# Linear attention and a two-layer feed-forward kernel: weight loads in another order, the first quarter of w_in used earlier, stage two reordered, q of batch 3 loaded two units later

## The chip, the core and the metric

The kernel runs on one core of a Trainium2 chip. Times are device microseconds of one execution. Five engines work side by side: TensorE (PE, matmuls; its weight loads are the row PEld), VectorE (DVE), ScalarE (ACT), GpSimd (POOL) and SyncE (SP). Here POOL issues nearly all loads, SP issues the DMA transposes and some of the stores. The metric is the time of the whole kernel, the median of the runs shown.

## What is computed

```python
def _attn_ref(q, k, v, g_norm):                      # batch 8, heads 8, sequence 576, head_dim 64
    kv = np.einsum('bhsd,bhse->bhde', k, v)
    out = np.einsum('bhsd,bhde->bhse', q, kv)
    rms = np.sqrt(np.mean(out * out, axis=-1, keepdims=True) + 1e-06)
    return (out / rms * g_norm).astype(np.float32)

def _moe_ref(x, w_in, w_out, alpha):                 # 4608 tokens, d_model 512, d_ff 2048
    h = x @ w_in
    g = np.maximum(h, 0.0) + alpha * np.minimum(h, 0.0)
    return (g @ w_out).astype(np.float32)

x = attn_out.transpose(0, 2, 1, 3).reshape(4608, 512)  # the attention's output is the input of the second part
```

All inputs and the output are float32; the kernel computes with float16 operands.

## The kernel before

**Tiling.** The 4608 tokens are cut into nine windows of 512 tokens (`NW = 9`, `W = 512`). A batch has 576 tokens, so windows and batches do not coincide. In each window the first matrix product has 16 groups (128 columns of w_in each, four matmuls of 512 tokens, `m1_mm`, L600). A group's result h in PSUM goes through ACT (`m1_neg`, L609) and DVE (`m1_sum`, L615), which together make the activation and leave it in SBUF as `gt`. The loop over windows 1 to 8 runs 16 units, one per group; other work is hung on unit numbers by tables.

**The second matrix product.** In window 0 it is plain: `y_run(a, (g,))` adds group g to token tile a (one matmul of 512 columns, L643). From window 1 on, the product with w_out is done in seven products of half size (Strassen's scheme in the form of Winograd): `X_LIST` holds products 1 and 2, `YZ_LIST` 6, 7, 4, 5 and 3. They need sums of blocks of `gt` (`s_sum`, DVE, the tables `S_ONE`, `S_TWO`, `S_ALL`, `S_LST` say in which unit) and sums of blocks of w_out (`w_sum`, DVE, made once). `X_AT`, `X_1`, `X_LAST`, `YZ_AT`, `YZ_1` say how many of the product matmuls (L796) are issued in each unit.

**Start and stage two.** Until about 18 us the kernel makes the attention of batch 0 for window 0, one pair of heads after the other: transpose q (`step_t`), make kv (`step_kv`), multiply (`step_ot`), sum the squares by a matmul (`ssq_mm`), scale (`norm`). `keep_warm` issues matmuls whose result nobody reads. The first group's matmuls for the first chunk of x (`m1_parts`) are already issued in between. Then come the 16 groups of window 0, then stage two: the y matmuls of window 0 in an order written out by hand, mixed with the attention of batch 1 (for window 1), with the scaling of w_in by g_norm (`scale_w_in`, needed from window 1 on) and with `w_sum`. [...]

**Rows.** From window 2 on, the attention of the next window is made by rows while a window runs: `rows_mm` (L499) multiplies for a tile of 128 tokens, `rows_sq`, `rows_rs` (ACT) and `rows_norm` (DVE, L580) scale it, and SP transposes the tile into `xt` by a DMA (L585). For tile 2 of window 2 a version by columns is used (`cols_mm`, `cols_norm`, L541), which needs no transpose. `ROW_AT[w]` gives the units, while window w-1 runs: `kv`, `mm`, the eight `sq`, and per tile `rs` and `norm`. A window's unit 0 issues its four matmuls first for the tokens of tiles 0 to 2 (384 columns, `m1_cols`, L631), then the other four for tile 3.

**Loads.** POOL issues the loads of weights, k, v and q. The DMA semaphores of this queue are a ring of eight: an issue waits until the load eight places ahead of it has landed. At the start the order of loads is written out by hand (`load0`, `load_w_in`, `load_w_out`, `load_main`, `load_rem`). w_in comes in six pieces (`IN_CUTS`): pieces 0 to 3 have 256 columns (groups 0 and 1, 2 and 3, 4 and 5, 6 and 7), pieces 4 and 5 have 512 (groups 8 to 11, 12 to 15); w_out comes in eight pieces of two groups each. Later loads hang on units by `LOADS`: for window w the tuple `q, k, v` gives the unit in which batch w+2 is loaded, and a `gate` makes POOL wait for the activation of the group of the unit before. So `(11, 1, 1)` for w = 1 means: k and v of batch 3 in unit 1 of window 1, q of batch 3 in unit 11 behind a gate on group 10. Batch 3's q is loaded by four issues of 128 KB (`load_q`) and one for the remaining 64 rows; SP transposes it (`dma_t`, L380) in unit 0 of window 2.

Of the kernel before, what the change touches and what calls it, by code (L numbers as in the profile page):

```python
# [9 lines left out]
FP32 = mybir.dt.float32  # L10
FP16 = mybir.dt.float16
# [6 lines left out]
def kernel(  # L18
# [11 lines left out]
    nc = tc.nc  # L30
# [5 lines left out]
    P = 128  # L36
# [186 lines left out]
    def load_w_in(i):  # L223
        f0, f1 = IN_CUTS[i], IN_CUTS[i + 1]
        t = w_p.tile([P, NC, f1 - f0], FP16, name=f"w_in_sb{i}")
        src = moe_w_in[:, f0:f1].rearrange("(c p) f -> p c f", p=P)
        for c in range(0, NC, NC // 2 if i == 0 else NC):
            n = NC // 2 if i == 0 else NC
            nc.gpsimd.dma_start(out=t[:, c : c + n, :], in_=src[:, c : c + n, :])
        w_in_sb.append(t)  # L230
# [38 lines left out]
    load0("k", 3)  # L269
    load0("v", 3)  # L270
    load_w_in(0)
    load_w_in(1)
    load_w_in(2)
    load_w_in(3)
    load_w_in(4)
    load_w_in(5)
    load_w_out(0)
    load_main(1, "k")
    load_w_out(1)
    load_rem(1, "k")  # L280
# [8 lines left out]
    load_rem(1, "q")  # L289
    load_w_out(6)  # L290
    load_w_out(7)

# [563 lines left out]
    X_AT = [0, 0, 0, 4, 1, 1, 1, 3, 1, 3, 2, 0, 2, 2, 1, 7, 2, 2]  # L856
    X_1 = [0, 0, 0, 0, 0, 0, 1, 0, 4, 0, 0, 0, 7, 4, 6, 8, 0, 2]
    X_LAST = [0, 0, 0, 2, 1, 2, 0, 1, 1, 1, 1, 0, 3, 4, 0, 0, 0, 0]
    YZ_AT = [3, 7, 6, 5, 5, 6, 7, 4, 5, 7, 5, 4, 5, 6, 5, 0]
    YZ_1 = [0, 8, 8, 5, 7, 4, 7, 5, 4, 6, 4, 6, 6, 5, 5, 0]  # L860
# [77 lines left out]
    keep_warm(1)  # L938
    norm(0, 1)
    step_kv(0, 3)  # L940
# [9 lines left out]
    first = [ps_h.tile([P, W], FP32, name="h_ps", tag="h1")]  # L950
    first += [ps_o.tile([P, W], FP32, name="h_ps", tag="o") for g in range(2)]
    ssq_mm(0, 2, h_at(0))
    for g in range(2):
        m1_parts(g, 0)
# [62 lines left out]
    y_run(2, (4,))
    scale_w_in(4, 3, 4, nc.scalar)
    scale_w_in(4, 1, 4, nc.scalar)
    scale_w_in(1)  # L1020
    scale_w_in(3)
    y_run(3, (6,))
    scale_w_in(2)
    y_run(2, (5,))
    step_t(1, 2, S_POOL)
    y_run(1, (7,))
    y_run(2, (6,))
    y_run(1, (6,))
# [18 lines left out]
    ssq_mm(1, 1, Q_POOL)
    y_run(0, (6,))
    y_run(0, (9,))
    norm(1, 0)  # L1050
    y_run(3, (9,))
# [38 lines left out]
    y_out(ys[1], 0, 1)  # L1090
    step_t_rem(1, Q_POOL)
# [23 lines left out]
    def row_kv(bs):  # L1115
# [26 lines left out]
        2, 3, 4, 5, 6, 8, 9), 'rs': (5, 5, 9, 12), 'norm': (5, 6, 9, 12), 'red': (0, 0, 0, 1)}}  # L1142
# [166 lines left out]
```

## Time and profile before

| what | us |
|---|---|
| runs shown: median (lowest to highest of 3) | 274.43 (274.05 to 274.45) |
| the profiled execution | 274.92 |
| its span, first to last instruction | 273.1 |
| PE busy | 265.7 (97%) |
| DVE busy | 217.3 (80%) |
| ACT busy | 156.4 (57%) |
| POOL busy | 87.6 (32%) |

The mean granted TensorE clock is 0.999. All times inside the kernel are counted from the start of the span. In the views by stretches a line has the stretch, its length, the busy time and number of instructions of PE, PEld, DVE, ACT and POOL, then the granted clock, the DMA share and the GB/s. In the timeline a line has start, length, engine, line of the kernel, operation, output and inputs, shape and count, and in brackets the idle time ahead of it and what ended it. Matmuls are pipelined: a 512-column matmul is shown as 0.38 us long, while the next one starts 0.216 us after it. In the list of DMA issues a line has the queue, the kind, the number of issues, the KB of each and the time from the issue to the landing of its last part.

### The profile page before, as it was taken

Reading aid. Unit: us, or ns where it says so; the run is one execution under the profiler, and the core shown is the slowest. Engines: PE = TensorE matmul, PEld = TensorE weight load, DVE = VectorE, ACT = ScalarE, POOL = GpSimd, SP = SyncE. Lnnn points to the kernel's source line nnn. Section 1 sums busy time; section 2 is a strip of 40 time slices with the busy share of each in tenths; the row PEclk is TensorE's granted clock in tenths of the full one; section 3 lists DMA queues with packets and bytes.
Section 4 is the critical chain, followed back from the end, with each engine's and each line's share of the span. In section 5 each row is a group of like instructions: output and inputs, shape, how many; then the busy total and the mean of one; then the engine's idle time right before and its main releaser. Section 6 shows DMA issues by size and latency. Waiting matters only on the chain.

```text
span 273.1 us, 6175 instructions
## 1 busy us (share of the span) xinstructions
PE 265.7 (97%) x2286; PEld 168.5 (62%) x2286; DVE 217.3 (80%) x413; ACT 156.4 (57%) x532; POOL 87.6 (32%) x134
## 2 busy tenths in 40 slices
PE   7899999999799999999999999999999999999995
PEld 3354444456566676666666666676666666666684
DVE  6459658999768986998699869986998889778964
ACT  3467576785468546764675468546854864443410
POOL 8773461606251545154514341440110011101100
PEclk9999999999999999999999999999999999999999
DMA  8999999999989899959995999595051122211123
GB/s 160 197 202 202 195 199 193 178 182 108 161 159 204 132 166 148 153 113 172 135 144 130 151 135 158 137 143 111 19 134 43 41 44 90 61 40 40 40 77 119
DMA packets 91571, 35.59 MB, mean 130 GB/s; under 512 B 62980, under 2 KB 89748, under 8 KB 91540
## 3 DMA queue, kind: packets, MB, share of 16 engines
q0 software_dynamic: 57872, 23.83, 69.1%
q1 hardware_dynamic: 32628, 10.34, 22.4%
q10 hardware_dynamic: 1040, 1.02, 1.2%
q8 instruction: 18, 0.29, 0.4%
q14 instruction: 13, 0.11, 0.2%
HBM read 36.71 MB, written 9.44 MB: 169 GB/s over the span
## 4 chain that ended last, share of the span: by engine, by line
PE 79%; DMA 14%; DVE 2%; issue 1%; POOL 1%; ACT 1%; POOLq 0%
PE h_ps L600 35%; PE yY L796 15%; PE yZ L796 9%; PE yX L796 9%; DMA w_out_sb<-in_moe_w_out_dram 5%; PE y L643 4%; DMA xt<-x_rows 4%; DMA w_in_sb<-in_moe_w_in_dram 3%; DMA qst<-in_q_dram 2%; PE h_ps L631 2%; PE kv_ps L1122 2%; PE or_ps L499 2%; DVE gt L615 1%; DVE x_rows L580 1%; PE yZ L791 1%
## 5 line engine op out<-in xcount | busy, mean ns | idle before, releaser
L600 PE MATMUL h_ps<-xt,w_in_sb 128*128 128x512 f16 x540 | 136.2, 379 | 0.0
L609 ACT ACTIVATE m_sb<-h_ps 128x512 f32<-128x512 f32 x144 | 86.7, 603 | 81.9 <-PE h_ps L600 61.4
L615 DVE SCALAR_TENSOR_TENSOR gt<-m_sb,beta_sb,h_ps 128x512 f16<-128x512 f32 x144 | 106.2, 743 | 24.1 <-ACT m_sb L609 21.3
L600 PEld LDWEIGHTS <-w_in_sb 128*128 128x128 f16 x540 | 51.2, 98 | 39.4 <-issue 0.2
L655 POOL DMA_DIRECT2D out_dram<-y_sb x32 | 20.6, 646 | 123.3 <-DVE y_sb L838 57.1
L796 PEld LDWEIGHTS <-s 128*128 128x128 f16 x496 | 48.3, 98 | 11.3 <-DVE s L733 0.3
L796 PEld LDWEIGHTS <-gt 128*128 128x128 f16 x384 | 37.5, 98 | 23.2 <-issue 0.2
L796 PE MATMUL yX<-w_out_sb,gt 128*128 128x256 f16 x256 | 44.6, 273 | 0.0
L796 PE MATMUL yY<-wsum,s 128*128 128x256 f16 x256 | 35.2, 273 | 0.0
L562 ACT ACTIVATE sq_sb<-or_ps 128x64 f16<-128x64 f32 x144 | 30.9, 256 | 2.6 <-PE or_ps L499 2.6
L562 ACT ACTIVATION_READ_ACCUMULATOR sq_sb<-or_ps 128x1 f32 x144 | 30.3, 242 | 0.0
L580 DVE TENSOR_TENSOR x_rows<-or_ps,rstd_r 128x512 f16<-128x512 f32 x27 | 18.4, 684 | 1.0 <-ACT rstd_r L572 1.0
L828 DVE TENSOR_TENSOR u<-yY,p 128x512 f32<-128x512 f32 x16 | 11.0, 689 | 9.0 <-PE yY L796 9.0
L185 POOL DMA_DIRECT2D qst<-in_q_dram x20 | 17.7, 901 | 1.0 <-issue 1.0
L796 PE MATMUL yY<-wsum,gt 128*128 128x256 f16 x128 | 17.6, 272 | 0.0
L796 PE MATMUL yZ<-wsum,s 128*128 128x256 f16 x120 | 17.5, 272 | 0.0
L796 PE MATMUL yZ<-w_out_sb,s 128*128 128x256 f16 x120 | 16.7, 273 | 0.0
L643 PE MATMUL y<-w_out_sb,gt 128*128 128x512 f16 x64 | 16.3, 379 | 0.1
L731 DVE TENSOR_TENSOR s<-gt 128x512 f16<-128x512 f16 x32 | 13.3, 418 | 0.1
L733 DVE TENSOR_TENSOR s<-s,gt 128x512 f16<-128x512 f16 x32 | 12.8, 420 | 0.4
L737 DVE TENSOR_TENSOR s<-gt,s 128x512 f16<-128x512 f16 x32 | 12.7, 418 | 0.0
L735 DVE TENSOR_TENSOR s<-gt 128x512 f16<-128x512 f16 x32 | 12.4, 417 | 0.0
(107 smaller groups left out, 233.1 us busy)
## 6 DMA issues: line engine op xcount, KB each, us to landing
out_dram<-y_sb POOLq DMA_DIRECT2D x16, 256.0 KB, 2.7
kst<-in_k_dram POOLq DMA_DIRECT2D x7, 512.0 KB, 8.0
vst<-in_v_dram POOLq DMA_DIRECT2D x6, 512.0 KB, 7.9
qst<-in_q_dram POOLq DMA_DIRECT2D x20, 128.0 KB, 4.5
w_out_sb<-in_moe_w_out_dram POOLq DMA_DIRECT2D x8, 256.0 KB, 10.9
out_dram<-y_sb SPq DMA_DIRECT2D x5, 256.0 KB, 2.6
w_in_sb<-in_moe_w_in_dram POOLq DMA_DIRECT2D x2, 512.0 KB, 9.9
qst<-in_q_dram POOLq DMA_DIRECT2D x2, 512.0 KB, 11.9
```

Source lines behind the costliest of these rows:

```text
L185: nc.gpsimd.dma_start(out=st[:, t, :, :], in_=srcs["q"][b, :, t * P : (t + 1) * P, :].rearrange("h p d -> p h d"),)
L562: nc.scalar.activation(out=sq[:, half, j], in_=o_ps[:, half, j], func=AF.Square, accum_out=ssq[:, half, j : j + 1],)
L580: nc.vector.tensor_tensor(out=xr[:].rearrange("p j h d -> p h j d"), in0=o_ps, in1=rstd[:].unsqueeze(3).to_broadcast([P, 2, NPAIR, D]), op ...
L600: nc.tensor.matmul(out=h_ps[:], lhsT=w_in_blk(c, g), rhs=xts[w][:, c, :], start=(c == 0), stop=(c == NC - 1),)
L609: nc.scalar.activation(out=neg[w, g][:], in_=h_ps[:], func=AF.Relu, scale=-1.0)
L615: nc.vector.scalar_tensor_tensor(out=gts[w, i][:, r, :], in0=neg.pop((w, g))[:], scalar=beta_sb[:, g : g + 1], in1=h_ps[:], op0=ALU.mult, ...
L643: nc.tensor.matmul(out=y[:], lhsT=gt_cols(w, g, a * P, (a + 1) * P), rhs=w_out_blk(g), start=(n == 1), stop=(n == NF),)
L655: engs[store_turn[0] % len(engs)].dma_start(out=dst, in_=src)
L731: nc.vector.tensor_add(out=t[:], in0=a21, in1=a22)
L733: nc.vector.tensor_sub(out=t[:], in0=sums[w, 1, k][:], in1=a11)
L737: nc.vector.tensor_sub(out=t[:], in0=a12, in1=sums[w, 2, k][:])
L796: nc.tensor.matmul(out=bank, lhsT=lhs, rhs=rhs, start=fresh, stop=(c == NK - 1), skip_group_check=True,)
```

## The change

- `load_w_in` takes the range of w_in's four row chunks that it loads. Piece 0 is loaded in three parts instead of two halves: the first quarter (chunk 0) goes between k and v of the last pair of batch 0 (pair 3), then chunk 1, then chunks 2 and 3.
- In the list of loads w_out's piece 0 goes ahead of w_in's piece 3, the remainder of k of batch 1 ahead of w_in's piece 5, and the remainder of q of batch 1 behind the last pieces of w_out.
- One `keep_warm(1)` is taken out. The two matmuls `m1_parts(1, 0)` go ahead of `step_kv(0, 3)`, in its place; `m1_parts(0, 0)` stays behind `ssq_mm(0, 2)`.
- Stage two: the same y matmuls, attention steps, scalings and sums in another order. Two of the three transposes that stood together stay together, the third and the fourth stand alone.
- Other unit numbers in the tables of products (`X_AT`, `X_1`, `X_LAST`, `YZ_AT`, `YZ_1`), of sums (`S_ONE`, `S_TWO`, `S_ALL`, `S_LST`) and of rows: in window 2's rows `norm` of tile 0 goes from unit 4 to 5, tile 2's `rs` from 10 to 11 and its `norm` from 13 to 14; in window 8's rows both `mm` go from unit 1 to 0; for windows 4 to 7 `rs` of tile 1 goes from 8 to 7.
- `LOADS`: q of batch 3 in unit 13 of window 1 instead of 11, its gate on group 12 instead of 10.

```diff
--- before.py
+++ after.py
@@ -220,14 +220,12 @@
     GW = NF // WQ
     IN_CUTS = [i * FW // 2 for i in range(4)] + [i * FW for i in range(2, WQ + 1)]
 
-    def load_w_in(i):
+    def load_w_in(i, cs=(0, NC)):
         f0, f1 = IN_CUTS[i], IN_CUTS[i + 1]
-        t = w_p.tile([P, NC, f1 - f0], FP16, name=f"w_in_sb{i}")
+        if cs[0] == 0:
+            w_in_sb.append(w_p.tile([P, NC, f1 - f0], FP16, name=f"w_in_sb{i}"))
         src = moe_w_in[:, f0:f1].rearrange("(c p) f -> p c f", p=P)
-        for c in range(0, NC, NC // 2 if i == 0 else NC):
-            n = NC // 2 if i == 0 else NC
-            nc.gpsimd.dma_start(out=t[:, c : c + n, :], in_=src[:, c : c + n, :])
-        w_in_sb.append(t)
+        nc.gpsimd.dma_start(out=w_in_sb[i][:, slice(*cs), :], in_=src[:, slice(*cs), :])
 
     def scale_w_in(i, h=0, n=1, eng=None):
         f = (IN_CUTS[i + 1] - IN_CUTS[i]) // n
@@ -267,17 +265,19 @@
     load0("k", 2)
     load0("v", 2)
     load0("k", 3)
+    load_w_in(0, (0, 1))
     load0("v", 3)
-    load_w_in(0)
+    load_w_in(0, (1, 2))
+    load_w_in(0, (2, 4))
     load_w_in(1)
     load_w_in(2)
+    load_w_out(0)
     load_w_in(3)
     load_w_in(4)
+    load_rem(1, "k")
     load_w_in(5)
-    load_w_out(0)
     load_main(1, "k")
     load_w_out(1)
-    load_rem(1, "k")
     load_main(1, "q")
     load_w_out(2)
     load_w_out(3)
@@ -286,9 +286,9 @@
     load_main(1, "v", HH, H)
     load_w_out(4)
     load_w_out(5)
-    load_rem(1, "q")
     load_w_out(6)
     load_w_out(7)
+    load_rem(1, "q")
 
     warm_ps = ps_q.tile([P, W], FP32, name="warm_ps", tag="q")
 
@@ -853,11 +853,11 @@
         return [(n, a * NK + c) for n in ns for c in range(NK) for a in range(2)]
 
     X_LIST, YZ_LIST = products(1, 2), products(6, 7, 4, 5, 3)
-    X_AT = [0, 0, 0, 4, 1, 1, 1, 3, 1, 3, 2, 0, 2, 2, 1, 7, 2, 2]
-    X_1 = [0, 0, 0, 0, 0, 0, 1, 0, 4, 0, 0, 0, 7, 4, 6, 8, 0, 2]
-    X_LAST = [0, 0, 0, 2, 1, 2, 0, 1, 1, 1, 1, 0, 3, 4, 0, 0, 0, 0]
-    YZ_AT = [3, 7, 6, 5, 5, 6, 7, 4, 5, 7, 5, 4, 5, 6, 5, 0]
-    YZ_1 = [0, 8, 8, 5, 7, 4, 7, 5, 4, 6, 4, 6, 6, 5, 5, 0]
+    X_AT = [0, 0, 0, 4, 1, 2, 1, 2, 0, 4, 2, 0, 2, 2, 1, 7, 2, 2]
+    X_1 = [0, 0, 0, 0, 0, 0, 1, 0, 4, 0, 0, 0, 6, 5, 6, 8, 0, 2]
+    X_LAST = [0, 0, 0, 2, 1, 2, 0, 0, 1, 2, 1, 0, 3, 4, 0, 0, 0, 0]
+    YZ_AT = [3, 7, 6, 5, 5, 6, 7, 4, 5, 7, 5, 4, 5, 7, 4, 0]
+    YZ_1 = [0, 9, 7, 5, 7, 4, 7, 4, 5, 6, 4, 6, 7, 5, 4, 0]
     YZ_WHAT = ("u2", "u3", "c21", "c22", "c12")
 
     def x_prods(w, u):
@@ -935,9 +935,7 @@
     ssq_mm(0, 1, h_at(2))
     step_t(0, 3, h_at(1), nc.vector.tensor_copy)
     step_ot(0, 2, (ps_y, "y"))
-    keep_warm(1)
     norm(0, 1)
-    step_kv(0, 3)
 
     def m1_parts(g, c, parts=(0, 1)):
         for i in parts:
@@ -947,11 +945,15 @@
                 start=(c == i == 0), stop=(c == NC - 1), skip_group_check=True,
             )
 
-    first = [ps_h.tile([P, W], FP32, name="h_ps", tag="h1")]
-    first += [ps_o.tile([P, W], FP32, name="h_ps", tag="o") for g in range(2)]
+    first = [
+        ps_h.tile([P, W], FP32, name="h_ps", tag="h1"),
+        ps_o.tile([P, W], FP32, name="h_ps", tag="o"),
+        ps_o.tile([P, W], FP32, name="h_ps", tag="o"),
+    ]
+    m1_parts(1, 0)
+    step_kv(0, 3)
     ssq_mm(0, 2, h_at(0))
-    for g in range(2):
-        m1_parts(g, 0)
+    m1_parts(0, 0)
     step_ot(0, 3, Q_POOL, 2)
     first.append(ps_s.tile([P, W], FP32, name="h_ps", tag="s"))
     norm(0, 2)
@@ -987,124 +989,124 @@
         for g in gs:
             y_mm(ys[a], 0, a, g)
 
+    y_run(3, (1,))
     y_run(0, (0,))
-    y_run(2, (0,))
-    y_run(3, (1,))
     y_run(1, (1,))
-    y_run(3, (2,))
     y_run(3, (3,))
     y_run(1, (2,))
     y_run(3, (0,))
+    scale_w_in(0)
     y_run(0, (1,))
-    scale_w_in(0)
     y_run(2, (2,))
+    y_run(2, (0,))
     y_run(2, (1,))
     w_sum(1, 0)
     y_run(0, (2,))
+    w_sum(1, 1)
+    y_run(1, (3,))
+    y_run(3, (2,))
+    step_t(1, 0, O_POOL)
+    step_t(1, 1, Q_POOL)
     y_run(2, (3,))
+    y_run(0, (3,))
     scale_w_in(4, 0, 4, nc.scalar)
     y_run(1, (0,))
-    w_sum(1, 1)
-    y_run(1, (3,))
-    y_run(0, (3,))
-    step_t(1, 0, S_POOL)
-    step_t(1, 1, Q_POOL)
     step_t(1, 3, O_POOL)
     y_run(3, (4,))
+    step_t(1, 2, S_POOL)
     y_run(0, (5,))
+    y_run(2, (4,))
+    scale_w_in(4, 3, 4, nc.scalar)
+    scale_w_in(2)
+    scale_w_in(1)
+    y_run(3, (5,))
+    y_run(2, (5,))
...
-    S_ALL = [(2, -1, 3, 0), (2, -1, 3, 1), (3, -1, 3, 2), (8, -1, 4, 2), (9, -1, 4, 3), (4, -1, 4,
-        0), (14, 0, 2, 0), (12, 0, 1, 1), (13, 0, 2, 1), (11, 0, 1, 0), (4, -1, 4, 1), (3, -1, 3,
-        3), (16, -1, 1, 3), (0, -1, 2, 2), (16, -1, 2, 3), (14, 0, 1, 2)]
-    S_ONE = [(6, 0, 3, 0), (11, 0, 3, 3), (13, 0, 3, 2), (4, 0, 3, 1)]
+    S_ALL = [(2, -1, 3, 0), (2, -1, 3, 1), (3, -1, 3, 2), (11, -1, 4, 3), (4, -1, 4, 0), (14, 0, 2,
+        0), (4, -1, 4, 1), (13, 0, 2, 1), (11, 0, 1, 0), (3, -1, 3, 3), (8, -1, 4, 2), (16, -1, 1,
+        3), (0, -1, 2, 2), (12, 0, 1, 1), (16, -1, 2, 3), (14, 0, 1, 2)]
+    S_ONE = [(7, 0, 3, 0), (13, 0, 3, 2), (10, 0, 3, 3), (4, 0, 3, 1)]
     S_TWO = [(2, -1, 4, 2), (0, -1, 1, 1), (0, -1, 1, 0), (0, -1, 2, 1), (16, -1, 1, 2), (0, -1, 2,
-        0), (16, -1, 2, 2), (16, -1, 1, 3), (12, 0, 1, 0), (4, -1, 4, 0), (6, -1, 4, 1), (9, -1, 4,
+        0), (16, -1, 2, 2), (16, -1, 1, 3), (12, 0, 1, 0), (3, -1, 4, 0), (6, -1, 4, 1), (9, -1, 4,
         3), (12, 0, 2, 0), (15, 0, 2, 1), (14, 0, 1, 2), (16, -1, 2, 3), (12, 0, 1, 1)]
     S_LST = [(0, -1, 2, 2), (2, -1, 3, 0), (9, 0, 3, 2), (2, -1, 3, 1), (3, -1, 3, 2), (6, -1, 4,
         0), (5, -1, 3, 3), (6, 0, 3, 0), (12, 0, 1, 1), (9, 0, 3, 1), (12, -1, 4, 2), (12, -1, 4,
-        3), (13, 0, 2, 0), (6, -1, 4, 1), (13, 0, 2, 1), (10, 0, 1, 0), (14, 0, 1, 2), (14, 0, 2,
-        2), (11, 0, 3, 3), (16, -1, 1, 3), (16, -1, 2, 3)]
+        3), (13, 0, 2, 0), (6, -1, 4, 1), (10, 0, 1, 0), (14, 0, 1, 2), (14, 0, 2, 2), (11, 0, 3,
+        3), (16, -1, 1, 3), (13, 0, 2, 1), (16, -1, 2, 3)]
 
     def unit_sums(w, u):
         at = S_ONE if w == 1 else S_TWO if w == 2 else S_LST if w == NW - 1 else S_ALL
@@ -1136,13 +1138,13 @@
                 )
 
     ROW_AT = {2: {'kv': 5, 'mm': {0: ((0,),), 7: ((1, 3),), 8: ((2,),)}, 'sq': (1, 1, 7, 7, 8, 10,
-        7, 8), 'rs': (3, 9, 10, 9), 'norm': (4, 9, 13, 9), 'red': (1, 1, 0, 1)}, 3: {'kv': 0, 'mm':
+        7, 8), 'rs': (3, 9, 11, 9), 'norm': (5, 9, 14, 9), 'red': (1, 1, 0, 1)}, 3: {'kv': 0, 'mm':
         {4: ((1, 0),), 5: ((3, 2),)}, 'sq': (4, 4, 5, 6, 8, 8, 8, 9), 'rs': (6, 6, 10, 11), 'norm':
-        (6, 7, 10, 11), 'red': (0, 0, 1, 0)}, 8: {'kv': 99, 'mm': {1: ((1, 0), (3, 2))}, 'sq': (1,
+        (6, 7, 10, 11), 'red': (0, 0, 1, 0)}, 8: {'kv': 99, 'mm': {0: ((1, 0), (3, 2))}, 'sq': (1,
         2, 3, 4, 5, 6, 8, 9), 'rs': (5, 5, 9, 12), 'norm': (5, 6, 9, 12), 'red': (0, 0, 0, 1)}}
     for w in range(4, B):
         ROW_AT[w] = {'kv': 2, 'mm': {4: ((1, 0), (3, 2))}, 'sq': (4, 4, 5, 6, 7, 7, 8, 10), 'rs':
-            (6, 8, 9, 11), 'norm': (6, 8, 9, 11), 'red': (0, 0, 1, 0)}
+            (6, 7, 9, 11), 'norm': (6, 8, 9, 11), 'red': (0, 0, 1, 0)}
     COL_TILES = ((2, 2),)
     ROWS = {"sq": rows_sq, "rs": rows_rs, "norm": rows_norm}
     COLS = {"sq": cols_sq, "rs": cols_rs, "norm": cols_norm}
@@ -1187,7 +1189,7 @@
 
     LOADS = {}
     for w in range(1, B - 2):
-        q, k, v = (11, 1, 1) if w == 1 else (12, 3, 5)
+        q, k, v = (13, 1, 1) if w == 1 else (12, 3, 5)
         for nm, at in (("q", q), ("k", k), ("v", v)):
             when = LOADS.setdefault((w + at // NF, at % NF), [])
             if at > 1 or w == 1:
```

More of the change, by code (lines that the diff above doesn't have):

```diff
@@ L1003 @@
     y_run(0, (2,))
+    w_sum(1, 1)
[3 more added lines that the diff above has]
+    step_t(1, 1, Q_POOL)
     y_run(2, (3,))
+    y_run(0, (3,))
     scale_w_in(4, 0, 4, nc.scalar)
     y_run(1, (0,))
-    w_sum(1, 1)
-    y_run(1, (3,))
-    y_run(0, (3,))
-    step_t(1, 0, S_POOL)
-    step_t(1, 1, Q_POOL)
     step_t(1, 3, O_POOL)
     y_run(3, (4,))
+    step_t(1, 2, S_POOL)
     y_run(0, (5,))
+    y_run(2, (4,))
[4 more added lines that the diff above has]
+    y_run(2, (5,))
+    scale_w_in(3)
+    y_run(2, (7,))
+    y_run(3, (6,))
+    scale_w_in(4, 1, 4, nc.scalar)
+    y_run(1, (6,))
+    y_run(1, (7,))
+    y_run(2, (6,))
     y_run(0, (4,))
     y_run(1, (4,))
[L1017 to L1028, printed above, removed]
+    step_kv(1, 0, O_POOL)
     scale_w_in(4, 2, 4, nc.scalar)
-    y_run(2, (7,))
-    y_run(3, (5,))
-    step_kv(1, 0, O_POOL)
+    y_run(1, (5,))
+    step_kv(1, 1, O_POOL)
+    y_run(0, (7,))
     for nm in ("k", "q"):
         nc.vector.memset(bufs[0][nm][REM:P, TPP, :, :], 0.0)
-    y_run(0, (7,))
-    step_kv(1, 1, S_POOL)
-    y_run(1, (5,))
+    step_ot(1, 0)
     y_run(3, (7,))
-    step_ot(1, 0)
     step_kv(1, 2)
@@ L1043 @@
     ssq_mm(1, 0, S_POOL)
+    y_run(0, (6,))
+    y_run(1, (8,))
+    ssq_mm(1, 1, Q_POOL)
+    y_run(0, (9,))
     y_run(0, (8,))
-    y_run(1, (8,))
+    y_run(3, (9,))
+    norm(1, 0)
     y_run(3, (8,))
[L1047 to L1051, printed above, removed]
+    w_sum(2, 0)
     norm(1, 1)
@@ L1054 @@
     step_ot(1, 2)
-    w_sum(2, 0)
-    w_sum(3, 1)
     y_run(2, (8,))
+    y_run(1, (10,))
     y_run(2, (9,))
     y_run(2, (11,))
-    y_run(1, (11,))
+    w_sum(3, 1)
+    ssq_mm(1, 2, S_POOL)
     y_run(1, (9,))
-    ssq_mm(1, 2)
-    y_run(2, (10,))
     y_run(2, (13,))
-    y_run(1, (10,))
+    y_run(0, (10,))
     w_sum(4, 0)
@@ L1068 @@
     y_run(0, (11,))
-    y_run(0, (12,))
-    y_run(0, (10,))
+    y_run(2, (10,))
     y_run(0, (13,))
     norm(1, 2)
-    w_sum(2, 1)
-    y_run(2, (12,))
+    y_run(0, (12,))
+    y_run(1, (11,))
     y_run(3, (12,))
@@ L1078 @@
     norm(1, 3)
+    y_run(2, (12,))
+    y_run(2, (14,))
+    w_sum(2, 1)
     y_run(1, (12,))
-    y_run(0, (14,))
+    y_run(1, (15,))
     w_sum(4, 1)
     y_run(2, (15,))
-    y_run(2, (14,))
     y_out(ys[2], 0, 2)
+    y_run(0, (14,))
     y_run(0, (15,))
-    y_run(1, (15,))
+    y_run(1, (14,))
     y_out(ys[0], 0, 0)
-    y_run(1, (14,))
+    step_t_rem(1, S_POOL)
     y_run(1, (13,))
     y_out(ys[1], 0, 1)
-    step_t_rem(1, Q_POOL)
     regroup(2, "q", 0, H)
```

## The prediction

> **What bounds the kernel now.** I read the page first (busy shares), then the stretches by stage, then the chain of waits and the PE timeline where PE stops, and last the DMA issues one by one. By stage (us; each engine's busy time; x is instructions):
>
> ```profile
> 16.20:29.12 12.92, 12.92 (x65) 6.19 (x64) 10.55 (x16) 9.50 (x17) 5.32 (x8) 1.00 1.36 201
> 29.12:47.50 18.38, 18.29 (x151) 8.83 (x149) 11.79 (x24) 11.34 (x20) 8.42 (x11) 1.00 1.45 197
> 47.50:67.90 20.40, 20.40 (x172) 11.01 (x170) 18.93 (x34) 15.03 (x31) 9.02 (x14) 1.00 1.40 157
> 67.90:69.80 1.90, 0.36 (x3) 0.10 (x1) 1.59 (x5) 0.00 (x0) 0.00 (x0) 1.00 2.26 150
> ```
>
> The first number after the length is PE. From 16.2 us PE never rests, at a granted clock of 1.00, until 67.9; from 70 us to the end it rests again only for some tenths. So an edit pays only where PE stands still, and costs only where it makes PE stand still. The one large stop is at 67.9, where window 2 begins:
>
> ```profile
> 67.45 0.81 PE L631 MATMUL h_ps<-xt,w_in_sb 128*128 128x384 f16 x4
> 69.83 0.38 PE L631 MATMUL h_ps<-xt,w_in_sb 128*128 128x128 f16 x4 [1.56 <-DMA xt<-x_rows]
> ```
>
> The first four matmuls use token tiles 0 to 2, the other four tile 3. The last of the first four starts at 67.93 and streams 384 columns (0.16), so PE is free at 68.09 and waits 1.73 us for tile 3. In the chain of waits:
>
> ```profile
> 60.80 1.28 DVE x_rows L580 x2
> ...
> 63.95 5.83 DMA xt<-x_rows
> ```
>
> Tile 3's rows are ready at 62.08, its transpose is issued at 63.95 and lands at 69.78. In the lists of DMA issues for short stretches (KB each, us to landing), at 55.7, 61.6, 64.0, 120.2 and 226.8 us:
>
> ```profile
> xt<-x_rows SPq DMA_TRANSPOSE x1, 8.9
> ...
> xt<-x_rows SPq DMA_TRANSPOSE x1, 3.5
> ...
> xt<-x_rows SPq DMA_TRANSPOSE x1, 5.8
> ...
> xt<-x_rows SPq DMA_TRANSPOSE x1, 3.8
> ...
> xt<-x_rows SPq DMA_TRANSPOSE x1, 2.4
> ```
>
> Alone a transpose lands after 2.4 us. With q loads issued just behind it (120.28 after 120.12) it takes 3.8. With q loads issued 0.6 us ahead of it (63.36, tile 3) 5.8, and behind half a megabyte of v and two stores 8.9. So POOL's loads that are ahead of a transpose hold it up.
>
> Before 50 us the loads come through POOL's queue one behind another at about 200 GB/s; a load lands when all ahead of it have. Issue times, and issue to landing of w_in piece 4, w_in piece 5 and w_out piece 0:
>
> ```profile
> 10.88 2.97 POOL L229 DMA_DIRECT2D w_in_sb<-in_moe_w_in_dram  x4 [1.17 <-DMA qst<-in_q_dram]
> 13.81 0.73 POOL L247 DMA_DIRECT2D w_out_sb<-in_moe_w_out_dram  x1
> ...
> w_in_sb<-in_moe_w_in_dram POOLq DMA_DIRECT2D x1, 512.0 KB, 9.0
> ...
> w_in_sb<-in_moe_w_in_dram POOLq DMA_DIRECT2D x1, 512.0 KB, 10.9
> ...
> w_out_sb<-in_moe_w_out_dram POOLq DMA_DIRECT2D x1, 256.0 KB, 11.5
> ```
>
> The four under L229 go at 10.88, 11.62, 12.35 and 13.08, so piece 4 lands at 21.38, piece 5 at 23.94, w_out 0 at 25.27: 512 KB take 2.56 us, 256 KB 1.33. In the same way piece 3 lands at 18.88, k of batch 1 at 27.90, w_out 1 at 29.14, the k remainder (64 KB) 0.46 later at 29.60, q at 32.29, w_out 2 and 3 at 33.55 and 34.80, the halves of v at 36.63 and 38.29.
>
> **The change part by part.** Every sum is made against the profiled execution: 274.92 us, span 273.1 and 1.8 around it. It lies 0.49 above the median 274.43, so I carry the difference over to the median.
>
> (a) First quarter of w_in. v of pair 3 (13.53) comes behind 64 KB more. 128 KB of w_in took 0.65, so it lands 0.33 later, at 13.86. On PE two 256-column matmuls replace one 512-column warm-up matmul, the same 0.22 us, so kv(0,3) has its place at 13.69 and starts at about 14.0, 0.14 behind the landing as before. It and the gap behind it last 0.31, and ssq(0,2), which now starts at 14.22 because it waits for ACT's square, starts at 14.31: +0.09. The chain behind it (ACT's rstd 0.69, squares 0.66, DVE's norm 0.75) holds PE until 16.16 in either version, so moving first-group matmuls forward gains nothing. Bounds 0 and +0.33. POOL gets one more issue, 0.7 us, some 5 us ahead of its landing. All of (a) vanishes in (b).
>
> (b) w_out 0 moves ahead of w_in 3, 4 and 5, and the k remainder ahead of 5. Landings: piece 3 at 18.88+1.33 = 20.21, and PE needs it for group 6 at 20.27 (weight load): just in time. Piece 4 at 21.38+1.33 = 22.71; PE needs it for group 8 at 22.00. With 0.05 for the semaphore and 0.09 from weight load to matmul, group 8 starts at 22.85 in place of 22.21: **+0.64**. Piece 5 at 25.27+0.46 = 25.73, needed at 25.45+0.64: in time. w_out 1 (set of loads ahead as for 29.60) is needed by the fourth y matmul at 29.76+0.65: in time. Bounds: 0, if the loads run a little faster, and 0.97, if piece 4 also carries the 0.33 of (a).
>
> (c) Stage two. 61 y matmuls, 32 transposes, kv, ot and ssq remain. Before, two transpose blocks stand between y matmuls (24 and 8 of them); after, three (16, 8, 8). A change between them costs about 0.1 us twice (the 8 block stands in 0.44, of which the transposes take 0.25): **+0.21**. Because everything comes 0.64 later, PE no longer waits for w_out 2 (0.13), w_out 3 (0.18) and the second v half (0.08): **-0.39**. By the landings above every other operand is there when its y matmul comes; norm(1,3) would be ready some 0.5 us ahead of window 1. Bounds: -0.39 with no price for the blocks, and +0.6 if one DVE operation (0.69: w_sum ahead of norm(1,1)) comes onto the path.
>
> (d) Window 1 and the stop at 68.09. The gate for q of batch 3 waits for group 12 in place of 10. Group 10's activation ends at 62.73; the q issue follows at 63.36. Group 12's ends at 64.38, so q starts at 64.95: 1.6 us later, 1.0 behind tile 3's transpose, like the 120 us case. The transpose then takes 3.8 at most and lands at 67.75, before 68.09: **-1.73**. Tile 2's norm goes one unit later; on DVE it stood at 65.57 behind a sum, now behind group 14's activation: that is ready at about 65.8 and ends at 66.57, the norm at 67.2, needed at 67.45: no cost, 0.2 us of cover. Tile 0's norm goes a unit later, 55.0 to about 55.9; it is needed at 67.45 and landed at 64.58. Bounds for (d): -1.73 and 0.
>
> (e) Behind q: q's loads land 1.6 us later, from 68.5 to about 70.1. SP waits there with its transposes of q, then the three late stores of y (75.4 to 79.7), then tile transposes that were issued at 84.18, 4.4 us after SP was free. First reader: PE's rows of window 3, at 78.07 before, at 76.8 after; the transpose issued at 68.66 landed after 5.0, so it would now land at about 75.5. The next reader comes 2 us later. Cost 0; the upper bound by the longest rows (6.8 for a q load, 5.9 for a transpose) is +0.8.
>
> (f) Other unit numbers (products, sums, ROW_AT 4 to 8). They move the same instructions between units in which PE is busy all the time (27.00 of 27.00 us from 72 to 99): 0. The small stop of 0.28 at 235.3, again for tile 3, may go or double: ±0.28.
>
> Sum: 0.64 + 0.21 - 0.39 - 1.73 = -1.27. 274.92 becomes 273.65, the median 274.43 becomes **273.2**.
>
> **The rivals.**
>
> Rival 1: q is only part of tile 3's delay. Transpose and loads share the engines fairly, so q at most doubled the time in which packets move, about 1.2 of the 2.4 us. Then 1.2 of the 5.8 goes and the rest has another cause: 0.53 of the stop stays, 273.7. For it: 61.5 us, a transpose with hardly any load in the queue, 3.5 and not 2.4. Against it: 8.9 behind v. The Trainium skill ("DMA: Bandwidth & Descriptors", "Queues, rings and completion order") states this rule: each engine takes turns between its queue rows, packet by packet. By that rule the time would be this rival's; the 8.9 us row disagrees with an even share, the 3.8 row agrees.
>
> Rival 2, the other side: SP's own queue decides. Tile 1's transpose held SP for 2.35 us (61.51 to 63.86, others 1.2) and thus set tile 3's issue, while tile 0's was still on its way to 64.58. If tile 0, now a unit (0.9) later, lands later, tile 1 holds SP as much longer and tile 3 starts up to 0.9 later, q again ahead of it. The stop stays and grows by some 0.4: -1.27+1.73+0.4 = +0.86, **275.3**. It decides from the point where tile 3 keeps PE for more than 1.27 us. Against it: tile 0's packets had to wait for v's load, whenever issued.
>
> Rival 3: q of batch 3 is too late, (e) at its upper bound: 274.0.
>
> Rival 4: stage two's new order or (b) costs 0.9 more: 274.1.
>
> **How the numbers follow.** 0.2% is 0.55 us, about what a measurement of this kernel can tell from no change. Forecast 0.52 (272.5 to 273.8), rival 1 0.12, both faster; rival 2 0.17, slower; rival 3 0.09, same; rival 4 0.10, 0.07 of it same and 0.03 slower. Faster 0.64, same 0.16, slower 0.20. Lower end: without (b) and its 0.39, with the 0.28 of (f), 272.6, so 272.5. The upper end 275.0 leaves out the worse part of rival 2.
>
> **What would show it.** In the new trace: group 8 of window 0 starts at about 22.85 behind piece 4's landing at 22.7; window 1 starts at about 47.9 (47.5 before); q's first issue comes about 1 us behind tile 3's transpose, which lands in under 4 us, and L631's second group follows the first without a stop; the rows of window 3 do not wait for qt_sb. Wrong: a stop at L631 again, for tile 3 or for tile 2's norm, a new one in front of the rows of window 3, or window 1 starting beyond 48.5.

## The result, and the profile after

The changed kernel takes 276.17 us (median of 6 runs, 275.27 to 276.64), the kernel before 274.44 (6 runs beside it): ratio 1.006, interval 1.0037 to 1.0082. It is slower by 1.0 to 2.3 us, where 1.2 less was predicted. Slow executions (966.18 and 1550.80 us, and two at 278.59 and 281.31 with a lower clock) are left out of all times and ratios. The profiled execution took 275.6 (span 273.8; before 274.92 and 273.1).

By stretches, the kernel after; the first number after the length is PE:

```profile
16.20:29.86 13.66, 12.59 (x61) 5.54 (x60) 10.88 (x17) 9.03 (x16) 5.79 (x8) 1.00 1.37 200
29.86:48.09 18.23, 18.23 (x151) 8.67 (x149) 11.21 (x22) 11.07 (x19) 7.72 (x10) 1.00 1.46 196
48.09:58.80 10.71, 10.71 (x109) 5.13 (x107) 10.22 (x20) 8.55 (x19) 4.52 (x8) 1.00 1.44 148
58.80:60.71 1.91, 0.17 (x2) 0.00 (x1) 1.91 (x4) 0.52 (x2) 0.00 (x0) 1.00 1.81 175
60.71:70.40 9.69, 9.69 (x61) 5.81 (x62) 7.28 (x13) 6.21 (x12) 3.06 (x5) 1.00 0.76 128
```

PE now stands still in two places: for 1.07 us in window 0 (first line), and for almost all of the 1.91 us from 58.80 on, in the middle of window 1, where it was busy before. The clock is 1.00 throughout. The PE timeline around these places and at the start of window 2:

```profile
20.42 1.90 PE L600 MATMUL h_ps<-xt,w_in_sb 128*128 128x512 f16 x8 [0.45 <-DMA w_in_sb<-in_moe_w_in_dram]
22.94 1.25 PE L600 MATMUL h_ps<-xt,w_in_sb 128*128 128x512 f16 x5 [0.62 <-DMA w_in_sb<-in_moe_w_in_dram]
...
60.71 0.40 PE L512 MATMUL oc_ps<-qt_sb,kv_masked 128*128 128x128 f16 x4 [1.74 <-DMA qt_sb<-qsb]
...
69.95 1.04 PE L631 MATMUL h_ps<-xt,w_in_sb 128*128 128x384 f16 x8
```

The last line is what step (d) wanted: L631's eight matmuls in one piece, no stop for tile 3 (the kernel before had 1.73). The first two are waits for w_in's pieces 3 and 4, ahead of groups 6 and 8. The third is new: `cols_mm` (L512), which makes tile 2 of window 2, waits for q of batch 2 in transposed form. Measured from matmul to matmul the stop is 1.91 us.

The chain of waits behind it:

```profile
49.15 0.61 ACT m_sb L609
49.76 1.10 SPq L380
...
50.90 1.59 SPq L380
...
52.54 8.13 DMA qt_sb<-qsb
...
60.71 0.40 PE oc_ps L512 x4
```

SP issues three transposes of q of batch 2 (`dma_t`, L380), at 49.56, 50.90 and 52.54. The third lands at 60.66, 8.1 us later. In the kernel before they went at 48.46, 49.80 and 51.11, and the third landed after 5.5, at 56.56, some 1.6 ahead of its reader. They wait for `regroup` (L209) on DVE. SP's longest wait, before and after (us in total, times, longest):

```profile
SPq L380 <- DVE qsb L209: 46.1, 1, 46.1
```

```profile
SPq L380 <- DVE qsb L209: 47.2, 1, 47.2
```

The first transpose went 0.1 behind the end of regroup in both; the chain names ACT's `m_neg` (L609) instead, but that ended at 49.76, when the transpose had already begun. DVE's timeline, before:

```profile
46.47 0.69 DVE L474 TENSOR_TENSOR xt<-ot_ps,rstd 128x512 f16<-128x512 f32 x1 [0.42 <-ACT rstd L464]
47.08 0.68 DVE L713 TENSOR_TENSOR wsum<-w_out_sb,wsum 128x1024 f16<-128x1024 f16 x1
47.68 0.68 DVE L209 COPY qsb<-qst 128x2048 f16<-128x2048 f16 x1
```

and after:

```profile
46.84 0.69 DVE L474 TENSOR_TENSOR xt<-ot_ps,rstd 128x512 f16<-128x512 f32 x1 [1.52 <-ACT rstd L464]
47.45 0.68 DVE L709 TENSOR_TENSOR wsum<-w_out_sb,wsum 128x1024 f16<-128x1024 f16 x1
48.17 0.69 DVE L713 TENSOR_TENSOR wsum<-w_out_sb,wsum 128x1024 f16<-128x1024 f16 x1
48.78 0.69 DVE L209 COPY qsb<-qst 128x2048 f16<-128x2048 f16 x1
```

L474 is `norm(1,3)`. The reordered stage two puts `w_sum(2,1)` (L709) behind it; before, it stood in the gap that DVE now spends idle (1.52). So regroup comes a full operation later behind the norm, besides the 0.4 by which the norm itself is later: 1.10 in all. The second transpose then held SP for 1.59 us (in the chain), 1.27 before, so the third went 1.43 later. POOL's load of k of batch 3, before and after, in its timeline:

```profile
51.18 0.91 POOL L176 DMA_DIRECT2D kst<-in_k_dram  x1
```

```profile
51.96 0.89 POOL L176 DMA_DIRECT2D kst<-in_k_dram  x1
```

This load hangs on a unit of window 1 and moved by 0.78 only. Before, the third transpose went 0.07 ahead of it; after, 0.58 behind it. My theory: that order is the loss.

### The profile page after: what moved, and what is told of

Same layout as the page of the kernel before. It is cut to its first block, busy times and chain, and to the rows that moved or that the text cites. A ratio compares the mean times of both kernels' runs of the same rounds, so it can differ in the third digit from the quotient of the medians.

```text
span 273.8 us, 6172 instructions
## 1 busy us (share of the span) xinstructions
PE 264.8 (97%) x2285; PEld 167.6 (61%) x2285; DVE 217.6 (79%) x413; ACT 156.8 (57%) x532; POOL 87.8 (32%) x135
## 3 DMA queue, kind: packets, MB, share of 16 engines
HBM read 36.71 MB, written 9.44 MB: 169 GB/s over the span
## 4 chain that ended last, share of the span: by engine, by line
PE 85%; DMA 10%; POOL 2%; SPq 1%; issue 1%; DVE 1%; ACT 0%; DVEq 0%; POOLq 0%
PE h_ps L600 39%; PE yY L796 15%; PE yX L796 10%; PE yZ L796 9%; PE y L643 5%; DMA w_in_sb<-in_moe_w_in_dram 4%; DMA qt_sb<-qsb 3%; PE h_ps L631 2%; DMA qst<-in_q_dram 2%; PE or_ps L499 1%; PE kv_ps L1124 1%; DMA out_dram<-y_sb 1%; SPq L380 1%; POOL w_in_sb L228 1%; PE qt_ps L336 0%
## 5 line engine op out<-in xcount | busy, mean ns | idle before, releaser
L609 ACT ACTIVATE m_sb<-h_ps 128x512 f32<-128x512 f32 x144 | 86.3, 600 | 81.2 <-PE h_ps L600 65.6
L796 PE MATMUL yX<-w_out_sb,gt 128*128 128x256 f16 x256 | 43.5, 273 | 0.0
L643 PE MATMUL y<-w_out_sb,gt 128*128 128x512 f16 x64 | 16.6, 380 | 0.0
```

Of the source, the lines that this page charges most:

```text
L609: nc.scalar.activation(out=neg[w, g][:], in_=h_ps[:], func=AF.Relu, scale=-1.0)
L643: nc.tensor.matmul(out=y[:], lhsT=gt_cols(w, g, a * P, (a + 1) * P), rhs=w_out_blk(g), start=(n == 1), stop=(n == NF),)
L796: nc.tensor.matmul(out=bank, lhsT=lhs, rhs=rhs, start=fresh, stop=(c == NK - 1), skip_group_check=True,)
```

## The experiments

Each set of runs has its own runs of the kernel before beside it (medians 274.05, 273.91, 274.08 and 274.17). "Third transpose" is its issue against the k load's (negative: ahead of it), and the time to its landing, from one trace each; "from w1" is the time from the first matmul of window 1 to the last matmul of the kernel.

| kernel | ratio (interval) | us | third transpose | lands after | stop ahead of L512 | from w1 |
|---|---|---|---|---|---|---|
| before (two traces) | 1 | | -0.07, -0.07 | 5.5, 5.6 | 0 | 222.67, 221.12 |
| after, again | 1.005 (1.0025 to 1.0076) | 275.35 | +0.74 | 8.1 | 2.07 | 222.75 |
| before, q in unit 13 | 0.9975 (0.9955 to 0.9995) | 273.34 | -0.07 | 5.4 | 0 | 220.67 |
| before, `w_sum` late | 1.0028 (1.0011 to 1.0045) | 274.71 | +0.23 | 7.8 | 1.42 | 222.17 |
| after, `w_sum` back | 1.0005 (0.9979 to 1.003) | 273.94 | +0.21 | 6.4 | 0 | 221.08 |
| after, loads back | 1.0042 (1.0017 to 1.0068) | 274.90 | +0.66 | 7.4 | 1.29 | 222.12 |
| after, both back | 1.0001 (0.9985 to 1.0017) | 274.22 | +0.19 | 7.0 | 0.18 | 220.86 |
| after, regroup early | 1.0011 (0.9986 to 1.0037) | 274.44 | -1.08 | 4.6 | 0 | 221.49 |
| after, k later | 1.0005 (0.998 to 1.003) | 274.24 | -2.33 | 3.7 | 0 | 220.70 |
| after, regroup early, q in 12 | 0.9997 (0.9982 to 1.0012) | 273.98 | -1.09 | 4.5 | 0 | 220.69 |
| before, q in 13, regroup early | 0.9965 (0.9943 to 0.9988) | 273.35 | -0.15 | 5.0 | 0 | 220.92 |
| the same, loads in the new order | 0.9967 (0.9955 to 0.9979) | 273.10 | 0.00 | 6.0 | 0 | 220.87 |

### Which part: q, the sum on DVE, or the loads

The kernel before with q alone:

```diff
-        q, k, v = (11, 1, 1) if w == 1 else (12, 3, 5)
+        q, k, v = (13, 1, 1) if w == 1 else (12, 3, 5)
```

> The kernel before with one change: q of batch 3 in unit 13 of window 1 (gate on group 12) instead of 11. Theory 1 (the prediction's step d: q's loads ahead of tile 3's transpose held it up): the first q issue goes behind tile 3's transpose, which lands in under 4 us; the stop of 1.73 us at L631 falls under 0.2; time 274.4 - 1.7 = 272.7. Rival (SP's own queue holds tile 3): the stop stays at 1.2 or more, time 274.0 or above. No stop in front of the oc_ps matmuls by either.

Measured 0.9975: faster by 0.7 us (1.7 expected), and no stop at L631 in the trace. Tile 3's transpose, in the list of DMA issues:

```profile
xt<-x_rows SPq DMA_TRANSPOSE x1, 2.4
```

The kernel before with the sum alone in its new place:

```diff
     norm(1, 2)
-    w_sum(2, 1)
...
     norm(1, 3)
+    w_sum(2, 1)
```

> The kernel before with one change: w_sum(2, 1) moved behind norm(1, 3), as in the changed kernel, so that it stands ahead of the regroup of q of batch 2. Theory 1 (DVE order): SP's first transpose starts 0.6 later (about 49.1), the third behind the k issue; a stop of 1 to 2 us appears in front of oc_ps; the stop at L631 stays near 1.7, since q and tile 3 move with PE; time 275.4 to 276.4. Rival (order of loads): no stop at oc_ps, time within 0.3 of 274.4.

Measured 1.0028, slower by 0.7 where 1.0 to 2.0 was expected, from moving one vector operation past another. Its PE timeline has the stop, with every load and all of PE's order as before:

```profile
59.41 0.38 PE L512 MATMUL oc_ps<-qt_sb,kv_masked 128*128 128x128 f16 x4 [1.25 <-DMA qt_sb<-qsb]
```

L631 had no stop in this trace although q stayed in unit 11, which the expectation had not seen. PE came there 1.2 us later than in the kernel before, and tile 3's transpose went at 64.10, this time ahead of q's first load (64.55).

The reverse, the changed kernel with the sum back behind `norm(1,2)`:

```diff
     norm(1, 2)
+    w_sum(2, 1)
...
     y_run(2, (14,))
-    w_sum(2, 1)
```

> The changed kernel with w_sum(2, 1) put back to where it stood, right behind norm(1, 2), ahead of norm(1, 3). Theory 1 (DVE order: one more w_sum of 0.6 us ahead of the regroup of q of batch 2 starts SP's three transposes so late that the third goes behind the k load of batch 3): SP's first transpose starts 0.6 earlier, at about 49.0, the third no later than 0.2 behind the k issue and lands before 58.5; the stop of 1.9 at the oc_ps matmuls is gone; profiled time 275.6 - 1.9 = 273.7. Rival (order of loads: the later start of window 1 alone does it): the stop stays at 1.5 or more and the time stays within 0.5 of 276.2.

Measured 1.0005, and no stop ahead of L512. The third transpose was still 0.21 behind the k load and took 6.4, not 8.1, which was just in time (57.90). So the loss hangs on tenths of a microsecond. And the sum is not all that makes the third late: here the first transpose went at 48.37, earlier than in the kernel before, but the second held SP for 1.76 us. In the six traces with the old stage two the second and third hold SP for 1.26 to 1.28 us; in all eight with the new one either the second or the third holds it for 1.5 to 1.8. Why stays open.

The changed kernel with the old order of w_out 0 and of the remainders of k and q:

```diff
-    load_w_out(0)
     load_w_in(3)
     load_w_in(4)
-    load_rem(1, "k")
     load_w_in(5)
+    load_w_out(0)
     load_main(1, "k")
     load_w_out(1)
+    load_rem(1, "k")
...
     load_w_out(5)
+    load_rem(1, "q")
     load_w_out(6)
     load_w_out(7)
-    load_rem(1, "q")
```

> The changed kernel with the loads of w_out 0, the k remainder and the q remainder back in the old order (the quarter of w_in stays). By step b of the prediction the stops in front of groups 6 and 8 (0.62 and 0.78 in the changed kernel's profile) go, so y starts 0.7 to 1.4 earlier. Theory 1 (DVE order): the regroup is still behind the extra w_sum, the third transpose still goes behind the k load, the stop at oc_ps stays at 1.0 or more; time about 275.2. Rival (order of loads): the stop at oc_ps goes too; time about 273.3.

Measured 1.0042: the stop stays (1.29), so the order of loads is not its cause. The waits for w_in are gone, yet window 1 started at 47.92, hardly earlier (48.09). Stage two has a wait of its own instead, for the transposes of batch 1:

```profile
32.59 0.64 PE L336 MATMUL qt_ps<-ident,qst 128*64 128x128 f16 x16 [0.50 <-DMA qst<-in_q_dram]
```

### The same stop from two other sides

The changed kernel once more:

> The changed kernel once more, to have it on one chip and against the same runs as its variants. Both theories: some 2 us above the version with w_sum(2,1) put back (273.94 against 274.05 for the kernel before), so about 275.9, ratio 1.005 to 1.009; a stop of 1.5 to 2.5 us ahead of cols_mm (L512) and none at L631.

Measured 1.005, with the stop at 2.07.

The sum left late, regroup moved ahead of it. Only this one operation moves, and only on DVE:

```diff
     norm(1, 3)
+    regroup(2, "q", 0, H)
...
-    regroup(2, "q", 0, H)
     w_sum(3, 0)
```

> The changed kernel with regroup(2, q) right behind norm(1,3) on DVE, ahead of both w_sums; w_sum(2,1) stays late, PE, ACT, POOL and SP keep their order. Theory (what counts is when SP's third transpose of q of batch 2 is issued against the k load of batch 3): regroup ends at about 48.2 instead of 49.5, SP then waits for ACT's copy (L367, ended at 48.55) and starts at about 48.6; the third transpose goes at about 51.2, 0.7 ahead of the k load (51.96), lands by 57, and the stop ahead of L512 is gone: about 1.9 less than the changed kernel, 273.9 to 274.3. Rival (w_sum's late place costs by itself, through what else is late on DVE): the stop stays or moves to the next operand, no more than 0.5 less than the changed kernel.

The third transpose went 1.08 ahead of the k load, and landed after

```profile
qt_sb<-qsb SPq DMA_TRANSPOSE x1, 4.6
```

No stop ahead of L512, and 0.9 us less than the changed kernel beside it; the rival, that the sum's place costs by itself, allowed 0.5. The forecast was 1.9. A part of the difference is a second stop, further on:

```profile
80.15 0.41 PE L499 MATMUL or_ps<-kv_masked,qt_sb 64*128 64x64 f16 x16 [0.62 <-DMA qt_sb<-qst]
```

Window 3's rows wait 0.79 (from matmul to matmul; 0.09 to 0.25 at this place in the other traces) for q of batch 3, which the change loads later. In the changed kernel itself PE and q's first load were both 1.7 us later (the load at 67.52, here at 65.85); there the third transpose of q took 5.7 us and was in time, here 6.8.

The cure from the load's side: the DVE order of the changed kernel, k and v one unit later:

```diff
-        q, k, v = (13, 1, 1) if w == 1 else (12, 3, 5)
+        q, k, v = (13, 2, 2) if w == 1 else (12, 3, 5)
```

> The changed kernel with k and v of batch 3 loaded in unit 2 of window 1 instead of 1, so the cure comes from the other side: the order on DVE stays as in the changed kernel, the load goes later. Theory: the k load is issued about 1 us later (53.2), 0.7 behind the third transpose (52.5), which lands at about 58 and not 60.7: at most 0.3 of the stop ahead of L512 is left, 1.3 to 2 less than the changed kernel, unless the later v then holds tile 0's or tile 3's transpose (64.3 and 67.7 in the trace of the changed kernel, needed at about 67.5 and 68.2), which would give up to 1 back. Rival (the transpose is slow whatever lies ahead of it, or the late regroup is what costs): the stop stays at 1.5 or more.

Now regroup and the transposes are as late as ever (the third at 53.40), but no k load is ahead:

```profile
qt_sb<-qsb SPq DMA_TRANSPOSE x1, 3.7
```

No stop, 1.1 us less than the changed kernel, where 1.3 to 2 was expected. (The k load went at 55.73, later than expected, because two stores of POOL came ahead of it.) So it is not the lateness of regroup that costs, but the load ahead; together with the run before, in which only regroup moved, this settles the order of the two issues as the cause of the stop.

### What remains of the loss

Without the stop the changed kernel is level with the kernel before, not 0.7 faster as with q alone. Five runs ask where that goes.

> The kernel before once more, for a second trace: my sum took the stop of 1.73 us at L631 from one execution, while q in unit 13 alone gained 0.7 us in the median. Theory (the stop differs from one execution to the next with the few tenths between the k load and the third transpose and between q and tile 3's transpose): a stop at L631 of another size, 0.3 to 1.5. Rival (the stop is always 1.7 and q in unit 13 costs 1 us elsewhere): again 1.6 to 1.8.

The stop at L631, in the kernel before's second trace:

```profile
68.36 0.38 PE L631 MATMUL h_ps<-xt,w_in_sb 128*128 128x128 f16 x4 [0.28 <-DMA xt<-x_rows]
```

It is 0.45 where the first trace had 1.73. Tile 3's transpose went 0.34 behind q's first load, not 0.59, and took 4.8, not 5.8. The theory's number held.

The changed kernel with the sum and the loads both back (the two diffs above together):

> The changed kernel with w_sum(2,1) right behind norm(1,2) again and the loads of w_out 0 and of the remainders of k and q in the old order: what is left of the change is the first quarter of w_in, the other order of stage two, the unit tables, and q in unit 13. Theory (lateness of the window's start by the loads, plus the third transpose, make up the whole loss): window 1 starts at 47.4 to 47.7, no stop ahead of L512 and none at L631, 273.2 to 273.6 as with q in unit 13 alone. Rival (stage two's order or the tables cost by themselves): 273.9 or more, with window 1 starting at 47.9 or later, as it did (47.92) with the loads alone put back.

Measured 1.0001, no stop at L631 and 0.18 at L512, but window 1 started at 48.78: the rival's numbers held. One part of that is a late start, which need not be the order's doing (the last pair's kv at 14.34, 13.7 on average with the quarter); the other is stage two, which took 18.90 us from first y matmul to window 1, not 18.38. In the PE timeline it waits as with the loads alone put back:

```profile
33.44 0.64 PE L336 MATMUL qt_ps<-ident,qst 128*64 128x128 f16 x16 [0.59 <-DMA qst<-in_q_dram]
```

So the new order of stage two, which asks for the first transposes of batch 1 three y matmuls sooner (behind 13, not 16), fits the new order of loads, where PE comes later, and costs with the old one.

Then the early regroup in the kernel before with q in unit 13:

```diff
     norm(1, 3)
+    regroup(2, "q", 0, H)
...
-    regroup(2, "q", 0, H)
```

> The kernel before with q of batch 3 in unit 13 and regroup(2, q) right behind norm(1,3). Theory: in the kernel with q alone the third transpose went only 0.07 us ahead of the k load, so that in some executions it falls behind; with regroup early SP is released by ACT's copy at 48.5 all the same, so the gain is small, 0 to 0.3 below 273.3, and the spread of the runs no larger. Rival: regroup was not what set SP, nothing changes: 273.3.

and on top of it the new order of loads, the load lines shown above the other way round:

> The kernel before with q of batch 3 in unit 13, regroup(2, q) early, and the loads of w_out 0 and of the remainders of k and q in the new order; w_in's piece 0 in two halves and stage two as before. Theory: PE stops ahead of group 6 or 8 of window 0 for 0.6 to 1.0 in all, y starts at 29.8 to 30.1 instead of 29.1 to 29.5, stage two gives at most 0.4 of it back: 0.4 to 0.9 above the same kernel with the old order of loads (273.35). Rival (stage two takes it all back, as PE then waits less for w_out and v): 273.2 to 273.5.

Early regroup gave nothing in time over q alone (0.9965 and 0.9975, the intervals overlap); SP is released by ACT's copy (L367) at about the same time, and the third transpose went 0.15 instead of 0.07 ahead of the k load. With the loads in the new order PE waits once for w_in:

```profile
22.58 1.68 PE L600 MATMUL h_ps<-xt,w_in_sb 128*128 128x512 f16 x7 [0.57 <-DMA w_in_sb<-in_moe_w_in_dram]
```

From the last pair's kv to the first y matmul it takes 16.18, against 15.43 or 15.44 in five traces of the kernel before and its variants; stage two then takes 18.08 instead of 18.38. In the trace that is 0.45 net, in time nothing that can be told (0.9967 and 0.9965), nearer to what the rival expected. With the first quarter moved as well, six traces of the changed kernel and its variants have 16.06 to 16.91 for the first of these (mean 16.58) and 18.23 or 18.24 for stage two: 1.0 net. The quarter is one issue more ahead of w_in's piece 1 in a ring of eight; that piece went at 10.05 to 10.87 instead of 8.74 to 9.44, and landed in two of the six traces at 17.2 to 17.3, with waits of 0.62 and 0.79 at 16.6 ahead of the first matmuls that read it. In the two runs with the quarter and the old loads that piece went at 10.76 and 11.20, so it is the quarter that delays it; but there the way from kv to y took 15.22 and 15.54, so with the old loads the quarter costs nothing that shows. No run has the new loads and stage two without the quarter, so its share in the 1.0 was not measured by itself.

The last run joins the early regroup with q between the two kernels' units:

```diff
-        q, k, v = (13, 1, 1) if w == 1 else (12, 3, 5)
+        q, k, v = (12, 1, 1) if w == 1 else (12, 3, 5)
```

> The changed kernel with regroup(2, q) right behind norm(1,3) and q of batch 3 in unit 12 of window 1, between the kernel before (11) and the changed kernel (13). With regroup early alone the trace showed no stop ahead of L512, but a new one of 0.79 us at 79.3: the third transpose of q of batch 3 went at 73.18 and landed at 80.02. Theory: q's first issue goes at about 65.0 instead of 65.85, still 0.9 behind tile 3's transpose (64.06), so L631 has no stop; q's transposes land about 0.9 earlier and the stop at 79.3 shrinks to 0.1 or goes: 273.5 to 273.9, 0.5 to 0.9 below regroup early alone (274.44 against 273.91 for the kernel before). Rival (the stop at 79.3 comes from something else than q's unit): 274.2 or more, the stop still 0.6 or more.

Measured 0.9997. Both stops are gone: from window 1 to the end it takes 220.69, like q alone; this fits the mechanism, though three versions with q in unit 13 have no second stop either. By the medians, each against the runs beside it, that is 0.7 below early regroup alone, but the two intervals overlap. The time itself (273.98) just missed the forecast of 273.5 to 273.9; the kernel before took 0.26 more beside it than in the set from which the forecast was made, and in the trace window 1 started at 49.01, 0.68 later than with early regroup alone.

Three versions beat both kernels: the kernel before with q in unit 13, 0.9975, with regroup early too, 0.9965, and with the new order of loads on top, 0.9967.

## Why the prediction was wrong, point by point

**(a) First quarter, +0.09: right for the step, incomplete.** The last pair's kv starts at 13.18 to 14.04 in six traces without it (mean 13.6) and at 13.22 to 14.34 in eight with it (mean 13.7). What the additional issue does to the pieces behind it in the ring of eight (piece 1 at 10.05 to 11.20, not 8.74 to 9.44) was not in the step.

**(b) w_in's piece 4, +0.64: right in kind, too small.** Groups 6 and 8 both waited, 0.62 and 0.78 us: piece 3, called "just in time", was not. With the new loads alone the step costs 0.75, with the quarter 1.15; the upper bound was 0.97. Window 1 starts at 48.09 (47.9 predicted), in six traces with the new loads and the quarter at 47.62 to 49.01.

**(c) Stage two, +0.21 - 0.39: right in size, and the step that failed.** It gave 0.15 back (0.18 predicted); with the new loads and the old order it is 0.30, so the new order costs 0.15 (0.21 predicted). But it only asked whether every y matmul finds its operand and whether window 1's own norm is in time. The moved `w_sum(2,1)` was looked at as a neighbour of the norms; that regroup stands behind it on DVE, SP's three transposes behind regroup, and that the third of them was 0.07 us ahead of a 512 KB load, is nowhere in the sum. This missing term measures 1.91 and 2.07 in the two traces of the changed kernel, and 0.9 to 1.4 in the medians of three versions that take it away (regroup early, k later, sum back). Its reader is ten microseconds and half a window further on, beyond where the step stopped looking.

**(d) The stop at L631, -1.73: right in mechanism, wrong in size.** q's first load went at 67.52, 2.2 behind tile 3's transpose, which landed after 2.4, and PE did not stop. But 1.73 was one execution's stop, another had 0.45, and q in unit 13 alone gains 0.7. The sum was carried over to the median as if the stop were the same in every execution; the profiled one lay 0.49 above the median, and this was its reason or part of it.

**(e) q of batch 3 too late, 0 to +0.8: 0 in the changed kernel, but a close race.** The third transpose of q lands at 80.42, its reader comes at 81.13. Of the four versions without the new stop and with q still in unit 13, three have it in time by 0.5 to 1.0 (sum back, both back, k later); in the fourth (regroup early) it took 6.8 us in place of 5.6 to 6.1, and PE waited 0.79, about the upper bound.

**(f) Tables: right at 0, but its ±0.28 was not the tables'.** From the first matmul of window 3 to the end, twelve of the fourteen traces take 173.02 to 173.09 us, whichever tables they have. The other two have window 8's stop for tile 3: the kernel before in its first trace (173.30), not in its second, and the changed kernel with the sum back (173.29). It is a stop of single executions.

**The rivals.** Rival 2 gave nearly this time (275.3), by chance, for its mechanism did not occur: L631 has no stop. It had the right resource, SP's transposes against POOL's loads, at the wrong place. Rival 1 is excluded by 2.4 us for tile 3; its 1.2 us of moving packets is 0.8 in the trace (the transpose alone, at 226.8). Rival 3's stop does not occur in the changed kernel, see (e). Of rival 4's 0.9 some 0.5 is there: the start costs 1.0 net in place of 0.46 (0.64 + 0.21 - 0.39).

The measured terms add up to +1.0 for the start, -0.7 for q and about +1.9 for the new stop, 2.2 us. The runs give 1.7 and 1.4. The start's and the stop's terms come from traces, which can differ from the median execution as in (d), so I leave the remaining 0.5 to 0.8 open.

## What to carry to other kernels

When an operation is moved on one engine, follow what now stands behind it to the next queue, and from there to the transfer it meets: a cover of 0.07 us between two DMA issues is no cover, whichever engine sets the one and the other. Do not book a stop at its full size from one profiled execution when its cause is such a close race; take a second trace first. The same holds for a transfer that is in time by some tenths, as q of batch 3 is here: in another execution it can be a stop, so give it a range and not a 0.

## What the runs showed of the hardware

The time of the same transpose of 128 rows, by its issue against the 512 KB load of k: 3.7 us with the load 2.3 behind it, 4.6 with 1.08 behind, 5.0 to 5.6 with 0.07 to 0.15 behind, 6.0 when both go at once, 6.4 to 7.8 when the load is 0.2 ahead, 7.4 to 8.1 at 0.6 to 0.7 ahead. So it grows steeply, by some 2 us within 0.3 to 0.7 us of issue time. I had expected that a load ahead holds it up, but not that this load's place within tenths decides.

Where the transpose was behind the load, both landed nearly together: 60.66 and 60.92 (transpose, load) in the changed kernel, 61.30 and 61.03 when it was run again, 59.37 and 59.72, 59.87 and 60.18, 59.63 and 60.23, 57.90 and 58.49 in the four variants; where it was ahead it landed 1.7 to 3.0 us sooner than the load (1.4 when both went at once, 5.2 with k one unit later).

The Trainium skill ("DMA: Bandwidth & Descriptors", "Queues, rings and completion order") says that a DMA's semaphore increment is a strongly ordered write, which lands only after every earlier write of that DMA engine, across its queues. The pairs agree with that.

The same section of the Trainium skill also states that each DMA engine takes turns between the queues, packet by packet. The packets in the two traces show that most of the additional time passes in such turns. The third transpose moves 512 packets of data. In the kernel before they go from 53.57 to 54.27 (q1 has SP's transposes, q0 POOL's loads; packets, MB, share of the 16 DMA engines):

```profile
q1 hardware_dynamic: 512, 0.13, 95.5%
q0 software_dynamic: 132, 0.03, 46.9%
```

In the changed kernel the same 512 go from 54.97 to 59.12, and with the transpose's last 32 small packets the view ends at 59.32:

```profile
q0 software_dynamic: 1161, 0.51, 106.5%
q1 hardware_dynamic: 544, 0.13, 41.3%
```

So 0.7 us have become some 4, and the load's packets go between those of the transpose, two for one and with four times the bytes. Even shares would have cost less: twice the 0.7 us would by my estimate have made 6.2 of the 5.5, where 8.1 was measured. Behind its last packet the transpose's landing comes 0.4 us later in the kernel before and 1.4 later in the changed one. So in these two traces what the order of the writes adds behind the packets is about 1 us at most, and no run shows it by itself; that part remains an explanation that fits.
